# Whole TensorE products cut into four column strips

## The chip, the cores and the metric

The kernel runs on one core of a Trainium2 chip. The metric is device time in microseconds (us), the median over several runs. The core has five engines that work in parallel: TensorE (PE, matrix products, with its own row PEld for the loading of weights), VectorE (DVE), ScalarE (ACT), GpSimd (POOL) and SyncE (SP, which starts transfers). Products land in PSUM, eight banks of 128 partitions by 512 fp32 values; everything else lies in SBUF.

## The reference

For one sequence of 2048 tokens with 512 features, `x`, the output is a gated mix of an attention block and an MLP block:

```python
g = _sigmoid((x * gate_w).sum(-1, keepdims=True))
a = _A_ref(x, A_wqkv, A_wo)                  # 32 heads of 16 features
b = _B_ref(x, B_w1, B_w2, B_w3, B_w4)
return g * a + (1 - g) * b

# _A_ref
scores = jnp.einsum("bhqd,bhkd->bhqk", q, k) * (Dh ** -0.5)
p = _softmax(scores, axis=-1)
o = jnp.einsum("bhqk,bhkd->bhqd", p, v)      # then @ wo

# _B_ref
h = _gelu(_layernorm(x, axis=-1) @ w1)
...                                          # four feature groups shifted by 1, -1, 2, -2 tokens
x1 = x + hs                                  # hs = shifted h @ w2
return x1 + _gelu(_layernorm(x1, axis=-1) @ w3) @ w4
```

## The kernel before

**Attention.** The work is cut into 32 units: four chunks of 512 queries (c) by eight groups of four heads (u). A unit has 64 blocks, one for each of 16 key tiles and four heads. A block is a score product (`score`, L709: 32 rows by 128 columns of the array, four of them beside each other in row tiles), an exp over 128x512 values, and a product with V (`attend_block`, L960: 128 rows by 17 columns, 16 features and a column of ones for the sum, 32 columns wide for the first key tile; four heads beside each other in column tiles of the array, the accumulator `acc` with one head in each quarter of the partitions).

**Who does the exps.** ScalarE does most: a slot is a stage in PSUM of two or three blocks, and one ACTIVATE (`expo`, L947) makes `pt` of it. The rest are done by VectorE with integer arithmetic on the bits of a float, in quads of four blocks (`whole`): a dump of each block out of `dsc` (L873), then the steps L883, L888, L893 and L898 on all four; three terms (`quad`, or a tile borrowed for it such as `more` or `xT`) go into the product with V.

**Whole products.** Everything else on TensorE uses the full array, 128 rows by 128 columns: the projections of q and k (`proj` by `bmm`, L223), of V (`v_proj`, L281), the MLP's four weights and the output projection (`bmm`, L223), the products of the gelu slots (`gelu_slot`, L723) and fills (`fill`, L1259 and L1262), which add zero to an accumulator and are there to be put where TensorE would otherwise have nothing to do.

**Order.** The order of all engines is made when the program is built, by a planner inside the kernel. It keeps an account of when each engine is free (`free`), of what each step costs, and picks the next step by rank and time. For TensorE a product costs `MM` = 0.2235 us, and a product whose kind (`state["kind"]`: score, attend, full) differs from the one before costs `TURN` = 0.09 us more. `fill` is chosen when the next step would start over 0.2 or 0.3 us later. `USUAL` and `RULES` hold, for each unit, when VectorE opens a quad and which unit's it is (NEED, AHEAD, DLIM, CHAINS), when its steps become urgent (HURRY), and when products with V go first (MANY, PTS). `AGE` says how fast a waiting VectorE step gains rank. On the chip each engine runs its list in this order, held together by semaphores, so the times are the chip's and only the order is the planner's.

The first 9 us (warm-up, transposes, first projections) and the last 9 us (`finish_range` and its products, L1106 to L1141) are written out apart from the planner's usual steps.

Of the kernel before, what the change touches and what calls it, by code (L numbers as in the profile page):

```python
# [32 lines left out]
def kernel(  # L33
# [13 lines left out]
    nc = tc.nc  # L47
    P = 128
    x_flat = A_x.flatten_outer_dims()
    out_flat = out.flatten_outer_dims()  # L50
    S, D = x_flat.shape
    H = 32
    DH = D // H
    KT = D // P
# [8 lines left out]
    CH = 512  # L63
# [30 lines left out]
    xT = [const.tile([P, KT, CH], BF16, name=f"xT{c}") for c in range(NC_)]  # L94
    wkv = wshare.tile([P, KT, 2 * D], BF16, tag="wshare", name="wkv")
    wq = const.tile([P, KT, D], BF16, name="wq")
# [7 lines left out]
    zero = const.tile([P, P], BF16, name="zero")  # L104
# [45 lines left out]
    for j in range(4):  # L150
        src = A_wo.rearrange("(G j a d) n -> j a d G n", j=4, a=2, d=DH)[j]
        for a in range(2):
            nc.sync.dma_start(
                out=wo_pad[32 * j + 1:32 * j + 1 + DH, :, :].rearrange("d (G a) n -> a d G n", a=2)[a],
# [3 lines left out]


    USUAL = {"NEED": 34, "AHEAD": 16, "HURRY": 14, "DLIM": 1.8, "MANY": 5, "PTS": 4, "CHAINS": 3}  # L160
    RULES = {1: {"NEED": 26, "HURRY": 0, "MANY": 5, "PTS": 6, "CHAINS": 3}, 2: {"NEED": 26, "HURRY": 0, "DLIM": 1.5, "MANY": 4, "PTS": 5}, 4: {"AHEAD": 16, "HURRY": 8}, 6: {"AHEAD": 6, "HURRY": 0, "DLIM": 2.1, "MANY": 4, "CHAINS": 4}, 7: {"MANY": 3, "PTS": 6}, 8: {"NEED": 26, "HURRY": 18, "CHAINS": 3}, 9: {"NEED": 36, "HURRY": 8, "DLIM": 2.1, "MANY": 3, "CHAINS": 5}, 10: {"DLIM": 1.2, "MANY": 5, "CHAINS": 4}, 12: {"NEED": 26, "HURRY": 18, "MANY": 2}, 13: {"HURRY": 8, "PTS": 5}, 14: {"NEED": 28, "AHEAD": 16, "HURRY": 24, "CHAINS": 5}, 15: {"AHEAD": 10, "MANY": 2, "PTS": 5}, 16: {"NEED": 28, "AHEAD": 16, "DLIM": 1.8, "MANY": 2}, 18: {"NEED": 30, "AHEAD": 6, "HURRY": 0, "MANY": 5}, 19: {"NEED": 32, "DLIM": 1.5}, 20: {"AHEAD": 8, "DLIM": 2.1, "MANY": 4, "PTS": 3, "CHAINS": 4}, 21: {"NEED": 32, "AHEAD": 16, "HURRY": 8, "PTS": 5}, 22: {"AHEAD": 8, "HURRY": 18, "MANY": 3, "PTS": 5}, 23: {"NEED": 30, "AHEAD": 12, "HURRY": 14, "DLIM": 2.1, "CHAINS": 4}, 24: {"NEED": 34, "AHEAD": 8, "MANY": 4, "PTS": 5}, 27: {"AHEAD": 10, "DLIM": 1.8, "CHAINS": 4}, 28: {"NEED": 26, "DLIM": 1.5, "MANY": 4}, 29: {"AHEAD": 10, "DLIM": 1.5, "MANY": 5, "CHAINS": 3}, 30: {"NEED": 28, "AHEAD": 10, "DLIM": 1.5, "MANY": 4}, 31: {"NEED": 32, "HURRY": 18, "MANY": 5, "PTS": 6, "CHAINS": 5}}
    MM = 0.2235
    TURN = 0.09
    PE_OUT = 0.43
    WARM = 8
    EARLY = 34
# [12 lines left out]
    FILL = 2  # L179
    DFILL = 1  # L180
    SLACK = 0.3
    AGE = 2.0
    ARANK = 3
    TANH = 1.5
    NOWFREE = 12.0
    free = {"pe": NOWFREE, "act": NOWFREE, "vector": NOWFREE, "pool": NOWFREE}
    queue = {"pe": [], "act": [], "vector": [], "pool": []}
    state = {"n": 0, "gen": 0, "young": True, "mm": 0, "kind": "", "t": 0.0, "piece": 0.0,
             "credit": 0.0, "mixable": 0, "done": False, "ending": False, "acc": 0.0, "accsb": 0.0, "slot": 0, "outs": 0, "bank": 0}
# [21 lines left out]
    def gen(name, dtype=F32):  # L211
# [5 lines left out]
            return psX.tile([P, CH], dtype, tag="x", name=name)  # L217
        return psG.tile([P, CH], dtype, tag="gen", name=name)

    def bmm(*args, **kwargs):  # L220
        state["mm"] += 1
        state["piece"] += MM
        nc.tensor.matmul(*args, **kwargs)  # L223

    def evac(cost, fn, test=None):

# [48 lines left out]
    def v_proj(t, half):  # L275
        c, o = divmod(t * P, CH)
        heads, width = slice(half * H // 2, (half + 1) * H // 2), D // 2
        yield all_at(("xT", c), "wv")
        ps = gen("ps_v")
        for kt in range(KT):  # L280
            nc.tensor.matmul(ps[:, 0:width], lhsT=xT[c][:, kt, o:o + P], rhs=wkv[:, kt, D + half * width:D + (half + 1) * width],  # L281
                             start=(kt == 0), stop=(kt == KT - 1))
            state["mm"] += 1
            state["piece"] += MM / 2 + 0.01
            if kt == 1:
                yield MM
        dst = vp0 if t == 0 else vp[t - 1]

        def fn(end):
            nc.vector.tensor_copy(out=dst[:, heads, 1:DH + 1], in_=ps[:, 0:width].rearrange("p (h d) -> p h d", d=DH))  # L290
            at["v", t, half] = end

        evac(0.42, fn)
        yield MM
# [283 lines left out]
    def job_run(start, job):  # L578

        if job == "out":  # L580
            job = Job(out_tile(*outs.popleft()))
        elif urgent and job is urgent[0]:
            urgent.popleft()
        state["t"] = start + (TURN if state["kind"] != "full" else 0.0)
        state["piece"] = 0.0
        try:
            v = next(job.steps)
        except StopIteration:
            current["job"] = job.hold = None
            state["done"] = state["done"] or job is main  # L590
            return
        if callable(v):
            current["job"], job.hold = None, v
            return
        current["job"] = job
        if not state["young"]:
            state["credit"] -= v
        free["pe"] = state["t"] + state["piece"]
        state["kind"] = "full"
# [15 lines left out]
    accs, stages, pts, old = {}, {}, {}, {}  # L615
# [97 lines left out]
    def gelu_slot(start):  # L713
        k = len(slots)
        item = turn[k] = gelus.popleft()
        _, _, _, w, rhs, ms, _, _ = item
        stages[k], _ = stage(k, False)
        slots.append([])
        state["slot"] = len(slots)
        state["mm"] = 0  # L720
        for i, m in enumerate(ms):
            for kt in range(KT):
                nc.tensor.matmul(stages[k][:, i * CH:(i + 1) * CH], lhsT=w[:, kt, m * P:(m + 1) * P], rhs=rhs[:, kt, :],  # L723
                                 start=(kt == 0), stop=(kt == KT - 1))
        free["pe"] = start + (TURN if state["kind"] != "full" else 0.0) + len(ms) * KT * MM
        state["kind"] = "full"
        scored[k] = free["pe"] - MM + PE_OUT

    def scores(start):
        k = len(slots)  # L730
        if gelus:
            return gelu_slot(start)
# [250 lines left out]
        return best  # L983

    def attend(start, source):
        begin = start + (TURN if state["kind"] != "attend" else 0.0)
        free["pe"] = begin + MM
        if source is waiting:
            n, kt, members, piece = waiting.popleft()
            if kt == 0:  # L990
                accs[n] = psA.tile([P, CH], F32, tag="acc", name="acc")
                state["acc"] = None
            for m in members:
                k, i = slot_of.pop((n, m) if piece is None else (n, m, piece))
                w = cut.get(k, CH)
                attend_block(n, m, pts[k][:, i * w:(i + 1) * w], r=piece)
                users[k] -= 1
                if users[k] == 0:
                    pt_free[k] = begin + PE_OUT
                    del pts[k]  # L1000
            if piece is not None:
                free["pe"] = begin + MM * w / CH
        else:

            free["pe"] = begin
            n = products[0][0]
            while products and products[0][0] == n and products[0][4] < free["pe"] + 0.02:
                _, kt, heads, term, _, ending = products.popleft()
                for r, j in enumerate(heads):
                    attend_block(n, 4 * kt + j, term.bitcast(BF16)[:, r, :], count=ending)  # L1010
                free["pe"] += MM
                freed[id(term)] = free["pe"] + 0.2
                room.append(term)
                due[n] -= 1
        state["kind"] = "attend"
        if n == len(units) - 1:
            for r in range(len(RANGES)):
                if left[n] == 0 and pieces[r] == 0:
                    pieces[r] = None
                    finish_range(r, free["pe"] - MM + PE_OUT)  # L1020
        elif left[n] == 0:
            finish_unit(n, free["pe"] - MM + PE_OUT)
# [169 lines left out]
    half = CH // 2  # L1192
# [61 lines left out]
    def fill(start):  # L1254

        state["mm"] += 1
        if accs:
            acc = list(accs.values())[0]
            nc.tensor.matmul(acc[:], lhsT=zero[:], rhs=wq[:, 0, :], start=False, stop=False, skip_group_check=True)  # L1259
        else:  # L1260
            spare = psG.tile([P, CH], F32, tag="gen", name="spare")
            nc.tensor.matmul(spare[:], lhsT=zero[:], rhs=wq[:, 0, :], start=True, stop=True)  # L1262
        free["pe"] = start + MM + (TURN if state["kind"] != "full" else 0.0)
        state["kind"] = "full"

    def option(e):
# [47 lines left out]
    while True:  # L1314
        options = []
        o = pe_option()
        if o:
            options.append((o[0], 0, "pe", o))
        for i, e in enumerate(("act", "vector", "pool")):
            o = option(e)  # L1320
# [4 lines left out]
        start, _, e, o = min(options, key=lambda x: x[:2])  # L1325
# [39 lines left out]
```

## Time and profile before

| | |
|---|---|
| median of 3 runs | 805.58 us (805.29 to 805.96) |
| span of the profiled execution | 803.7 us |
| between span and median | 1.9 us; no other time of the profiled execution is given |
| TensorE products, weight loads | 6332 and 6332, busy 773.4 us and 245.8 us |
| VectorE, ScalarE | busy 760.8 us and 787.6 us |
| mean granted TensorE clock | 0.997 |
| first exp starts, last exp ends | 9.0 us, 794.9 us |

How to read it: the page shares out the span by engine, and names the chain of work that ended last. A busy TensorE is no proof of a full one, since the end of a product is modelled and products overlap: what counts is the distance from one start to the next. In a group of instructions, the number behind the second bar is the idle time of the engine just before them, with what ended it.

### The profile page before, as it was taken

How to read it: one execution, taken by the hardware profiler on the slowest of the kernel's cores; microseconds unless marked ns; L12 is line 12 of the kernel's file. 1: busy time of each engine (PE TensorE's matmuls, PEld its weight loads, DVE VectorE, ACT ScalarE, POOL GpSimd, SP SyncE). 2: the span in 40 equal slices, each digit the busy share in tenths (PEclk: the TensorE clock that was granted, in tenths of full speed). 3: DMA queues.
4: the chain of work that ended last, by engine and by line, in shares of the span. 5: the costliest groups of instructions: out<-in, count | busy, mean ns of one | idle time of the engine just before them, and what ended most of it. 6: DMA issues, size and time to landing. Idle time of an engine off the chain costs nothing.

```text
span 803.7 us, 15774 instructions
## 1 busy us (share of the span) xinstructions
PE 773.4 (96%) x6332; PEld 245.8 (31%) x6332; DVE 760.8 (95%) x1237; ACT 787.6 (98%) x734; POOL 19.6 (2%) x46
## 2 busy tenths in 40 slices
PE   9999999999999999999999999999999999999997
PEld 3333333332322323232222233222233233322223
DVE  5799999999889999999999997999999999999995
ACT  6999999999999999999999999999999999999996
POOL 4100000000000000010000000000000000000000
PEclk9999999999999999999999999999999999999998
DMA  8700031230100033001000001001001000000000
GB/s 201 179 15 15 16 67 28 41 42 15 42 1 15 15 106 42 15 1 41 15 14 26 18 15 41 15 3 42 13 14 41 15 6 12 21 21 29 15 15 27
DMA packets 48176, 26.41 MB, mean 33 GB/s; under 512 B 34664, under 2 KB 43624, under 8 KB 48104
## 3 DMA queue, kind: packets, MB, share of 16 engines
q1 hardware_dynamic: 47144, 24.90, 13.0%
q8 instruction: 49, 0.80, 0.4%
q10 hardware_dynamic: 960, 0.52, 0.2%
q14 instruction: 23, 0.19, 0.1%
HBM read 17.04 MB, written 2.35 MB: 24 GB/s over the span
## 4 chain that ended last, share of the span: by engine, by line
ACT 59%; issue 21%; PE 17%; DVE 2%; DVEq 0%; ACTq 0%
ACT pt L947 54%; PE stage L709 5%; PE acc L960 4%; PE ps L223 3%; ACT g2T L925 2%; ACT g2T L928 1%; DVE st L311 1%; ACT L925 1%; PE ps_y L223 1%; PE acc L1259 1%; ACT hT L925 1%; PE ps_v L281 1%; PE ps_k L223 1%; PE warm L1177 0%; PE spare L1262 0%
## 5 line engine op out<-in xcount | busy, mean ns | idle before, releaser
L947 ACT ACTIVATE pt<-stage 128x1024 bf16<-128x1024 f32 (+1 forms) x695 | 738.1, 1236 | 2.6 <-PE stage L709 1.2
L709 PE MATMUL stage<-qT,kT 32*128 32x512 bf16 (+2 forms) x1644 | 270.9, 379 | 22.1 <-ACT pt L947 10.8
L873 DVE TENSOR_SCALAR quad<-dsc 128x512 int16<-128x512 f32 x320 | 213.2, 684 | 13.7 <-PE dsc L709 11.8
L709 PE MATMUL dsc<-qT,kT 32*128 32x512 bf16 x428 | 164.5, 384 | 0.0
L960 PE MATMUL acc<-pt,vp 128*17 128x512 bf16 (+3 forms) x1644 | 157.1, 380 | 1.1 <-ACT pt L947 0.8
L709 PEld LDWEIGHTS <-kT 32*128 32x128 bf16 x2072 | 83.5, 91 | 237.1 <-issue 203.8
L960 PEld LDWEIGHTS <-vp 128*17 128x17 bf16 (+1 forms) x2928 | 60.3, 88 | 131.4 <-issue 119.4
L960 PE MATMUL acc<-quad,vp 128*17 128x512 bf16 x884 | 82.7, 382 | 0.3
L1259 PE MATMUL acc<-wq,zero 128*128 128x512 bf16 x216 | 75.9, 387 | 0.0
L223 PE MATMUL ps<-w,g2T 128*128 128x512 bf16 x224 | 68.4, 384 | 0.8 <-DVE x_sb L433 0.8
L898 DVE TENSOR_SCALAR quad<-quad 128x2048 int16<-128x2048 int16 x80 | 54.2, 679 | 0.3
L223 PE MATMUL ps_y<-xnT,w 128*128 128x512 bf16 x176 | 54.1, 384 | 0.1
L873 DVE TENSOR_SCALAR xT<-dsc 128x512 int16<-128x512 f32 x60 | 40.0, 684 | 0.7 <-PE dsc L709 0.4
L888 DVE TENSOR_TENSOR quad<-quad,quad 128x2048 bf16<-128x2048 bf16 x30 | 36.4, 1213 | 0.3
L883 DVE TENSOR_SCALAR quad<-quad 128x2048 int16<-128x2048 int16 x50 | 34.2, 683 | 0.1
L893 DVE TENSOR_SCALAR quad<-quad 128x2048 int16<-128x2048 int16 x50 | 34.1, 682 | 0.1
L873 DVE TENSOR_SCALAR more<-dsc 128x512 int16<-128x512 f32 x48 | 32.2, 686 | 0.9 <-PE dsc L709 0.2
L1259 PEld LDWEIGHTS <-zero 128*128 128x128 bf16 x216 | 19.1, 96 | 44.8 <-issue 41.6
L223 PEld LDWEIGHTS <-g2T 128*128 128x128 bf16 x224 | 16.9, 97 | 33.1 <-issue 27.5
L723 PE MATMUL stage<-xnT,w 128*128 128x512 bf16 x112 | 25.0, 379 | 0.1
L960 PE MATMUL acc<-more,vp 128*17 128x512 bf16 x248 | 24.3, 382 | 0.0
L1031 DVE COPY accsb<-acc 128x512 f32<-128x512 f32 x31 | 21.2, 684 | 1.6 <-PE acc L960 1.3
(145 smaller groups left out, 682.0 us busy)
## 6 DMA issues: line engine op xcount, KB each, us to landing
bcs<-rec_d SPq DMA_DIRECT2D x31, 256.0 KB
w<-in_B_w_dram SPq DMA_DIRECT2D x2, 1792.0 KB
out_dram<-ot SPq DMA_DIRECT2D x15, 128.0 KB
x_sb<-in_A_x_dram SPq DMA_DIRECT2D x14, 128.0 KB
w<-in_B_w_dram SPq DMA_DIRECT2D x2, 512.0 KB
wkv<-in_A_wqkv_dram SPq DMA_DIRECT2D x1, 512.0 KB
wo_pad<-in_A_wo_dram SPq DMA_DIRECT2D x8, 64.0 KB
xnT<-xn SPq DMA_TRANSPOSE x32
```

The source lines that it names most:

```text
L223: nc.tensor.matmul(*args, **kwargs)
L709: nc.tensor.matmul(out, lhsT=kT[G][32 * j:32 * j + 32, cc, o:o + P], rhs=qTs[(c, G)][32 * j:32 * j + 32, a, lo:hi], start=True, stop=True, ...
L723: nc.tensor.matmul(stages[k][:, i * CH:(i + 1) * CH], lhsT=w[:, kt, m * P:(m + 1) * P], rhs=rhs[:, kt, :], start=(kt == 0), stop=(kt == KT ...
L873: nc.vector.tensor_scalar(out=bits[:, r, :], in0=dsc[:], scalar1=SHIFT, scalar2=LOWEST, op0=ALU.add, op1=ALU.max)
L883: nc.vector.tensor_scalar(out=tiles["once"], in0=bits, scalar1=0x7F, scalar2=0x3F00, op0=ALU.bitwise_and, op1=ALU.bitwise_or)
L888: nc.vector.tensor_tensor(out=tiles["twice"].bitcast(BF16), in0=bits.bitcast(BF16), in1=tiles["once"].bitcast(BF16), op=ALU.mult)
L893: nc.vector.tensor_scalar(out=tiles["once"], in0=bits, scalar1=0x7F80, scalar2=None, op0=ALU.bitwise_and)
L898: nc.vector.tensor_scalar(out=bits, in0=bits, scalar1=QUARTER, scalar2=None, op0=ALU.add)
L925: nc.scalar.activation(out=part, in_=part, func=ACT.Gelu_apprx_tanh)
L947: nc.scalar.activation(out=pt[:, 0:w], in_=stages.pop(k)[:, 0:w], func=ACT.Exp, scale=LN2 / 128.0)
L960: nc.tensor.matmul(accs[n][32 * j:32 * j + M, lo:hi], lhsT=lhsT, rhs=p, start=(kt == 0), stop=(kt == NT - 1), skip_group_check=True, tile_ ...
L1259: nc.tensor.matmul(acc[:], lhsT=zero[:], rhs=wq[:, 0, :], start=False, stop=False, skip_group_check=True)
```

## The change

A new helper `strips` issues a whole product as four products of 32 columns, each with its own 32 columns of weights and its own quarter of the output's partitions, and with the tile position of that column strip. `bmm`, `v_proj`, `gelu_slot` and `fill` use it. The head and the tail keep their whole products, and so do the small gate products. The planner's account then charges no turn between whole products and products with V (`NARROW`), `AGE` is doubled, and some units have other rules. The planner makes a new order of that.

```diff
-    RULES = {... 4: {"AHEAD": 16, "HURRY": 8}, 6: {... "MANY": 4, "CHAINS": 4}, 7: {"MANY": 3, "PTS": 6}, ... 9: {"NEED": 36, ...
+    RULES = {... 4: {"AHEAD": 16, "HURRY": 8, "CHAINS": 6}, 6: {... "MANY": 8, "CHAINS": 2}, 7: {"MANY": 3, "PTS": 6, "CHAINS": 6}, ... 9: {"NEED": 24, ...
...
+    NARROW = ("full", "attend")
...
-    AGE = 2.0
+    AGE = 4.0
...
+    def strips(out, lhsT, rhs, **kwargs):
+
+        for j in range(0, P, 32):
+            nc.tensor.matmul(out[j:j + 32, :], lhsT=lhsT[:, j:j + 32], rhs=rhs, tile_position=(0, j), **kwargs)
+
     def bmm(*args, **kwargs):
         state["mm"] += 1
         state["piece"] += MM
-        nc.tensor.matmul(*args, **kwargs)
+        strips(*args, **kwargs)
...
         for kt in range(KT):                                                     # v_proj
-            nc.tensor.matmul(ps[:, 0:width], lhsT=xT[c][:, kt, o:o + P], ...
+            strips(ps[:, 0:width], lhsT=xT[c][:, kt, o:o + P], ...
...
-        state["t"] = start + (TURN if state["kind"] != "full" else 0.0)          # job_run
+        state["t"] = start + (TURN if state["kind"] not in NARROW else 0.0)
...
             for kt in range(KT):                                                 # gelu_slot
-                nc.tensor.matmul(stages[k][:, i * CH:(i + 1) * CH], lhsT=w[:, kt, m * P:(m + 1) * P], ...
+                strips(stages[k][:, i * CH:(i + 1) * CH], lhsT=w[:, kt, m * P:(m + 1) * P], ...
...
-        begin = start + (TURN if state["kind"] != "attend" else 0.0)             # attend
+        begin = start + (TURN if state["kind"] not in NARROW else 0.0)
...
-            nc.tensor.matmul(acc[:], lhsT=zero[:], rhs=wq[:, 0, :], start=False, ...      # fill
+            strips(acc[:], lhsT=zero[:], rhs=wq[:, 0, :], start=False, ...
```

The rules also change in units 16, 21, 23, 24, 26, 27, 28, 29 and 30 (for example unit 27, AHEAD from 10 to 4). `gelu_slot` and `fill` charge the turn by `NARROW` as well.

More of the change, by code (lines that the diff above doesn't have):

```diff
@@ L160 @@
     USUAL = {"NEED": 34, "AHEAD": 16, "HURRY": 14, "DLIM": 1.8, "MANY": 5, "PTS": 4, "CHAINS": 3}
-    RULES = {1: {"NEED": 26, "HURRY": 0, "MANY": 5, "PTS": 6, "CHAINS": 3}, 2: {"NEED": 26, "HURRY": 0, "DLIM": 1.5, "MANY": 4, "PTS": 5}, 4: {"AHEAD": 16, "HURRY": 8}, 6: {"AHEAD": 6, "HURRY": 0, "DLIM": 2.1, "MANY": 4, "CHAINS": 4}, 7: {"MANY": 3, "PTS": 6}, 8: {"NEED": 26, "HURRY": 18, "CHAINS": 3}, 9: {"NEED": 36, "HURRY": 8, "DLIM": 2.1, "MANY": 3, "CHAINS": 5}, 10: {"DLIM": 1.2, "MANY": 5, "CHAINS": 4}, 12: {"NEED": 26, "HURRY": 18, "MANY": 2}, 13: {"HURRY": 8, "PTS": 5}, 14: {"NEED": 28, "AHEAD": 16, "HURRY": 24, "CHAINS": 5}, 15: {"AHEAD": 10, "MANY": 2, "PTS": 5}, 16: {"NEED": 28, "AHEAD": 16, "DLIM": 1.8, "MANY": 2}, 18: {"NEED": 30, "AHEAD": 6, "HURRY": 0, "MANY": 5}, 19: {"NEED": 32, "DLIM": 1.5}, 20: {"AHEAD": 8, "DLIM": 2.1, "MANY": 4, "PTS": 3, "CHAINS": 4}, 21: {"NEED": 32, "AHEAD": 16, "HURRY": 8, "PTS": 5}, 22: {"AHEAD": 8, "HURRY": 18, "MANY": 3, "PTS": 5}, 23: {"NEED": 30, "AHEAD": 12, "HURRY": 14, "DLIM": 2.1, "CHAINS": 4}, 24: {"NEED": 34, "AHEAD": 8, "MANY": 4, "PTS": 5}, 27: {"AHEAD": 10, "DLIM": 1.8, "CHAINS": 4}, 28: {"NEED": 26, "DLIM": 1.5, "MANY": 4}, 29: {"AHEAD": 10, "DLIM": 1.5, "MANY": 5, "CHAINS": 3}, 30: {"NEED": 28, "AHEAD": 10, "DLIM": 1.5, "MANY": 4}, 31: {"NEED": 32, "HURRY": 18, "MANY": 5, "PTS": 6, "CHAINS": 5}}
@@ new lines @@
+    RULES = {1: {"NEED": 26, "HURRY": 0, "MANY": 5, "PTS": 6, "CHAINS": 3}, 2: {"NEED": 26, "HURRY": 0, "DLIM": 1.5, "MANY": 4, "PTS": 5}, 4: {"AHEAD": 16, "HURRY": 8, "CHAINS": 6}, 6: {"AHEAD": 6, "HURRY": 0, "DLIM": 2.1, "MANY": 8, "CHAINS": 2}, 7: {"MANY": 3, "PTS": 6, "CHAINS": 6}, 8: {"NEED": 26, "HURRY": 18, "CHAINS": 3}, 9: {"NEED": 24, "HURRY": 8, "DLIM": 2.1, "MANY": 3, "CHAINS": 5}, 10: {"DLIM": 1.2, "MANY": 5, "CHAINS": 4}, 12: {"NEED": 26, "HURRY": 18, "MANY": 2}, 13: {"HURRY": 8, "PTS": 5}, 14: {"NEED": 28, "AHEAD": 16, "HURRY": 24, "CHAINS": 5}, 15: {"AHEAD": 10, "MANY": 2, "PTS": 5}, 16: {"NEED": 30, "AHEAD": 16, "DLIM": 1.8, "MANY": 2}, 18: {"NEED": 30, "AHEAD": 6, "HURRY": 0, "MANY": 5}, 19: {"NEED": 32, "DLIM": 1.5}, 20: {"AHEAD": 8, "DLIM": 2.1, "MANY": 4, "PTS": 3, "CHAINS": 4}, 21: {"NEED": 32, "AHEAD": 16, "HURRY": 8, "PTS": 5, "CHAINS": 6}, 22: {"AHEAD": 8, "HURRY": 18, "MANY": 3, "PTS": 5}, 23: {"NEED": 30, "AHEAD": 12, "HURRY": 14, "DLIM": 1.2, "CHAINS": 4}, 24: {"NEED": 34, "AHEAD": 8, "MANY": 5, "PTS": 5}, 26: {"NEED": 36}, 27: {"AHEAD": 4, "DLIM": 1.8, "CHAINS": 4}, 28: {"NEED": 26, "DLIM": 1.5, "MANY": 4, "PTS": 6, "AHEAD": 20}, 29: {"AHEAD": 10, "DLIM": 1.5, "MANY": 5, "CHAINS": 3, "PTS": 4}, 30: {"NEED": 28, "AHEAD": 10, "HURRY": 18}, 31: {"NEED": 32, "HURRY": 18, "MANY": 5, "PTS": 6, "CHAINS": 5}}
@@ L280, in v_proj @@
         for kt in range(KT):
-            nc.tensor.matmul(ps[:, 0:width], lhsT=xT[c][:, kt, o:o + P], rhs=wkv[:, kt, D + half * width:D + (half + 1) * width],
+            strips(ps[:, 0:width], lhsT=xT[c][:, kt, o:o + P], rhs=wkv[:, kt, D + half * width:D + (half + 1) * width],
                              start=(kt == 0), stop=(kt == KT - 1))
@@ L722, in gelu_slot @@
             for kt in range(KT):
-                nc.tensor.matmul(stages[k][:, i * CH:(i + 1) * CH], lhsT=w[:, kt, m * P:(m + 1) * P], rhs=rhs[:, kt, :],
+                strips(stages[k][:, i * CH:(i + 1) * CH], lhsT=w[:, kt, m * P:(m + 1) * P], rhs=rhs[:, kt, :],
                                  start=(kt == 0), stop=(kt == KT - 1))
-        free["pe"] = start + (TURN if state["kind"] != "full" else 0.0) + len(ms) * KT * MM
+        free["pe"] = start + (TURN if state["kind"] not in NARROW else 0.0) + len(ms) * KT * MM
         state["kind"] = "full"
@@ L1258, in fill @@
             acc = list(accs.values())[0]
-            nc.tensor.matmul(acc[:], lhsT=zero[:], rhs=wq[:, 0, :], start=False, stop=False, skip_group_check=True)
+            strips(acc[:], lhsT=zero[:], rhs=wq[:, 0, :], start=False, stop=False, skip_group_check=True)
         else:
             spare = psG.tile([P, CH], F32, tag="gen", name="spare")
-            nc.tensor.matmul(spare[:], lhsT=zero[:], rhs=wq[:, 0, :], start=True, stop=True)
-        free["pe"] = start + MM + (TURN if state["kind"] != "full" else 0.0)
+            strips(spare[:], lhsT=zero[:], rhs=wq[:, 0, :], start=True, stop=True)
+        free["pe"] = start + MM + (TURN if state["kind"] not in NARROW else 0.0)
         state["kind"] = "full"
```

## The prediction

> **What bounds the kernel now.** I read the page first: busy shares and the chain that ended last.
>
> ```profile
> span 803.7 us, 15774 instructions
> ...
> PE 773.4 (96%) x6332; PEld 245.8 (31%) x6332; DVE 760.8 (95%) x1237; ACT 787.6 (98%) x734; POOL 19.6 (2%) x46
> ...
> ACT 59%; issue 21%; PE 17%; DVE 2%; DVEq 0%; ACTq 0%
> ```
>
> Three engines look full, and 38% of the chain (issue 21, PE 17) lies on TensorE, which invites the thought that a cheaper TensorE shortens the run. So next come the stretches between the first and the last exp (the first two windows below are the whole of the head and of the middle), the ACTIVATEs by form, and the waits.
>
> ```profile
> core 0: us, PE busy (x) PEld busy (x) DVE busy (x) ACT busy (x) POOL busy (x), PEclk, DMA share, GB/s
> 0.00:9.00 9.00, 7.70 (x48) 3.93 (x48) 3.65 (x10) 2.64 (x5) 8.10 (x34) 1.00 0.69 179
> 9.00:795.00 786.00, 760.63 (x6258) 239.00 (x6261) 753.21 (x1218) 784.01 (x728) 10.27 (x13) 1.00 0.13 31
> 795.00:803.70 8.70, 5.05 (x30) 2.84 (x29) 3.91 (x11) 0.96 (x2) 1.26 (x1) 0.76 0.17 60
> 486.79:488.40 1.61, 1.61 (x33) 0.71 (x32) 0.01 (x1) 1.61 (x2) 0.00 (x0) 1.00 0.39 127
> 787.25:795.12 7.87, 7.03 (x114) 3.25 (x113) 3.29 (x8) 7.64 (x7) 0.00 (x0) 1.00 0.01 2
> ```
> ```profile
> L947 ACT ACTIVATE pt<-stage 128x1024 bf16<-128x1024 f32 x465 | 441.7, 1095 | 1.9 <-PE stage L709 1.2 <-PE dsc L709 0.2 <-ACT pt L947 0.2
> L947 ACT ACTIVATE pt<-stage 128x1536 bf16<-128x1536 f32 x230 | 321.5, 1519 | 0.7
> ```
> ```profile
> PE stage L709 <- ACT pt L947: 10.8, 38, 0.8
> ```
>
> From 9 to 795 us ScalarE is busy 784.0 of 786.0 us. Before all 695 exps together it stood idle 1.9 + 0.7 = 2.6 us, while TensorE's scores waited 10.8 us for it. ScalarE is the bound, and TensorE follows it. The idle figure is a little low:
>
> ```profile
> 399.40 5.75 ACT L947 ACTIVATE pt<-stage 128x1024 bf16<-128x1024 f32 x6
> ```
>
> Six exps of 1024 columns take 5.75 us; less the last one's 1.10, the starts are 0.93 us apart, though each is 1.10 long. A delay under 0.17 us is thus covered by the overlap and shows nowhere. My estimate of all waits of ScalarE is 4.0 us: the 2.6 of the row and about half as much again of hidden ones. That is everything a faster TensorE can win.
>
> **The change, part by part.** The sum is made against the profiled execution: a span of 803.7 us, with 1.9 us around it up to the runs' median of 805.58. I carry those 1.9 us along and count in medians.
>
> *ScalarE's own work.* Counted in the two programs' instruction lists, the exps stay 695, but 465 of two blocks and 230 of three become 461 and 234: four more blocks on ScalarE, and 107 quads by VectorE become 106. By the rows above a third block costs 1519 - 1095 = 424 ns: 4 x 0.424 = **+1.70 us**, on the path. Gelus and table loads keep their numbers. VectorE gets one quad less, four dumps and four steps,
>
> ```profile
> L873 DVE TENSOR_SCALAR quad<-dsc 128x512 int16<-128x512 f32 x320 | 213.2, 684 | 13.7 <-PE dsc L709 11.8
> L898 DVE TENSOR_SCALAR quad<-quad 128x2048 int16<-128x2048 int16 x80 | 54.2, 679 | 0.3
> L888 DVE TENSOR_TENSOR quad<-quad,quad 128x2048 bf16<-128x2048 bf16 x30 | 36.4, 1213 | 0.3
> ```
>
> 4 x 0.684 + 3 x 0.68 + 1.213 = 6.0 us. It was idle 33 us in the middle, so this gains nothing by itself.
>
> *TensorE's turns.* The timeline of TensorE alone shows what a change of tiling costs:
>
> ```profile
> 399.71 0.39 PE L709 MATMUL stage<-qT,kT 32*128 32x512 bf16 x2
> 399.72 0.38 PE L709 MATMUL dsc<-qT,kT 32*128 32x512 bf16 x1
> 400.03 0.39 PE L960 MATMUL acc<-more,vp 128*17 128x512 bf16 x4
> 400.25 0.39 PE L960 MATMUL acc<-pt,vp 128*17 128x512 bf16 x4
> 400.57 0.39 PE L709 MATMUL stage<-qT,kT 32*128 32x512 bf16 x2
> 400.58 0.38 PE L709 MATMUL dsc<-qT,kT 32*128 32x512 bf16 x1
> 400.89 0.39 PE L960 MATMUL acc<-quad,vp 128*17 128x512 bf16 x4
> 401.22 0.39 PE L223 MATMUL ps<-w,g2T 128*128 128x512 bf16 x1
> 401.54 0.39 PE L709 MATMUL stage<-qT,kT 32*128 32x512 bf16 x2
> ```
> ```profile
> 785.77 0.82 PE L1259 MATMUL acc<-wq,zero 128*128 128x512 bf16 x3
> ```
>
> V after V starts 0.22 us later (400.03 to 400.25); score to V, V to score, V to whole and whole to score each take 0.32 or 0.33 us. Whole after whole is (0.82 - 0.39) / 2 = 0.215 us (785.77). So each turn costs about 0.105 us more than a product of the same tiling. In the lists, neighbours of different tiling number 1758 before; after it 1380, since a strip product and a V product both tile 128x32. That removes 378 x 0.105 = 40 us of TensorE. The list has 64 fills more (288 for 224): 64 x 0.215 = 14 us back. Net about **-26 us of TensorE**, all beside ScalarE's work. TensorE's needs in the lists are, before, 557 us of products (0.216 us each, narrower ones pro rata) and 1758 x 0.106 = 186 us of turns, 744 us; after, 571 + 146 = 717 us, beside ScalarE's 786. Nothing of it counts directly; it counts where TensorE was late for ScalarE. Between two scores TensorE's work, fills left out, exceeded the exp's time (0.92 us for two blocks, 1.34 for three, estimates from the spacing above and the 0.424) in 251 of 683 slots of the list; after the change in 160 of 679, and slots with over 1.3 us of work fall from 64 to 17. The first count says 36% fewer waits, the second 73%. I take half: **-2.0 us** of the 4.0.
>
> *A strip's own price.* No whole product stands in strips in this trace. The nearest rows are V's four tiles, 17 or, for the first block, 32 columns wide:
>
> ```profile
> 67.64 0.61 PE L960 MATMUL acc<-pt,vp 128*32 128x512 bf16 x8
> ```
> ```profile
> 486.79 1.40 PEld L960 LDWEIGHTS <-vp 128*17 128x17 bf16 x32 [0.42 <-issue]
> ```
> ```profile
> L960 PEld LDWEIGHTS <-vp 128*17 128x17 bf16 x2800 | 58.5, 88 | 121.8 <-issue 110.0 <-DVE accsb L1093 0.8 <-DVE st L311 0.5
> L960 PEld LDWEIGHTS <-vp 128*32 128x32 bf16 x128 | 3.4, 93 | 9.6 <-issue 9.4 <-DVE vp L290 0.2
> L223 PEld LDWEIGHTS <-g2T 128*128 128x128 bf16 x224 | 16.9, 97 | 33.1 <-issue 27.5
> ```
>
> Four 32-column tiles and the next four take 0.61 - 0.39 = 0.22 us, like a whole product, loads included. A 32-column load takes 93 ns, a 128-column one 97, and the four stand almost together. I therefore take a strip product at 0.22 us and its four loads at nothing: the running product covers them. If that cover is gone, each product bears up to 0.093 us (a rival). Below nothing it can't go: the same 512 columns stream through every tile.
>
> [...]
>
> *Instructions.* Each of the 1264 strip products (fills among them) issues eight instructions for two; the list grows from 12,664 to 20,360. On average one must leave every 786 / 20,200 = 39 ns. Rows: eight V products in a row, 65 instructions in 1.61 us, or 25 ns each; 227 in 7.87 us, 35 ns each, over the longest dense stretch. Taken at nothing, with the bound as a rival. Waits and semaphore steps stay as many (1451 matmuls wait, 1455 before), and no DMA is added or moved out of its queue by the strips; AGE and the rules only shift when jobs and quads fall. Head and tail (9.0 and 8.7 us) keep their whole products.
>
> Sum: 805.58 + 1.70 - 2.0 = **805.3 us**.
>
> **The rivals.**
>
> *Nearly every wait goes.* If TensorE is never late, all 4.0 us go: 805.58 + 1.70 - 4.0 = 803.3 us. For it: the 26 us freed, and 17 crowded slots for 64. Against: the 160 that stay, and waits at table changes and unit ends that are VectorE's.
>
> *The turn stays* (it ends slower). If strip and V still drain each other, because their loads cannot pass, the 403 strip-V neighbours of the new list bear 0.105 us that its account leaves out: 42 us, TensorE at 759 of 786. Still not the bound on average, but late in the crowded slots: 160 x 403/679 x 0.105 = 10 us of lateness, of which I let half reach ScalarE past its second buffer: with +1.70, 812 us. It decides from the point where ScalarE's waits do not shrink at all, 807.3 us. For it: 17 columns next to whole strips isn't in the trace. Against: 32-column V next to 17-column V runs without a turn.
>
> *The issue of instructions binds.* At 40 ns each, 20,360 take 814 us, and with head and tail 832 us. It decides above 39 ns. Against: 25 and 35 ns in the rows; for it: both stretches are short, and instructions queued ahead may flatter them. [...]
>
> *Loads are not covered.* 1264 x 0.093 = 118 us on TensorE, 717 + 118 = 835, with head and tail 853 us. It decides when over (786 - 717) / 1264 = 55 ns of each are exposed. Against: the V rows.
>
> **How the numbers follow.** Some of the waits go, 805.3 us: 0.41, its own range 804.0 to 807.1. Nearly all go: 0.27. The turn stays, or the new order makes ScalarE wait as long as before or longer: 0.20. Issue binds: 0.09. Loads uncovered: 0.03. What a measurement here can tell from no change is about 0.2%, 1.6 us: 804.0 to 807.2. So faster 0.27, same 0.41, slower 0.20 + 0.09 + 0.03 = 0.32. The range 803.0 to 811.0 takes in the second case and most of the third, and leaves out the last two and the third's upper end.
>
> **What would show it.** Right: strip to V and V to strip 0.22 us apart; strip to strip 0.22; TensorE's scores waiting more than 10.8 us for exps; ScalarE's idle before the exps under 2.6 us; ScalarE's middle stretch near 786 us again. Wrong: strip to V at 0.32 (the turn stays), strip to strip above 0.25 with loads starting late (issue or loads), or idle before the exps of 4 us and more with PE as its releaser. If the exps' idle falls to nearly nothing and the span is still near 804, the bound was read rightly and the gain simply had no room.

## The result, and the profile after

The changed kernel takes 812.93 us (median; 811.68 to 813.63) where the kernel before took 805.77 us beside it: a ratio of 1.0086 [1.0073 to 1.0099], about 7 us slower. The profiled execution of after took 813.63 us. The lines below answer to those of before. First the page: span, busy shares with the number of instructions, and the chain that ended last.

```profile
span 811.7 us, 23471 instructions
...
PE 767.6 (95%) x10180; PEld 267.8 (33%) x10180; DVE 757.6 (93%) x1229; ACT 789.7 (97%) x734; POOL 19.1 (2%) x46
...
ACT 60%; issue 22%; PE 15%; DVE 2%; DMA 0%; DVEq 0%; ACTq 0%
```

TensorE's busy time fell by 6 us although it now issues 3800 products more, and VectorE's by 3 us. The span grew by 8.0 us. Next the stretches up to the first exp, between the first and the last, and after it, and one dense stretch.

```profile
core 0: us, PE busy (x) PEld busy (x) DVE busy (x) ACT busy (x) POOL busy (x), PEclk, DMA share, GB/s
0.00:9.53 9.53, 8.31 (x48) 4.64 (x48) 3.55 (x10) 2.63 (x4) 8.63 (x35) 1.00 0.72 187
9.53:803.85 794.32, 755.56 (x10102) 261.07 (x10103) 750.03 (x1209) 786.15 (x728) 9.19 (x11) 1.00 0.13 31
803.85:811.70 7.85, 3.78 (x31) 2.09 (x30) 4.04 (x12) 0.96 (x2) 1.27 (x1) 1.00 0.19 67
15.66:81.77 66.11, 64.01 (x1000) 25.55 (x1001) 60.71 (x127) 65.87 (x67) 4.35 (x6) 1.00 0.29 81
```

The middle is 8.3 us longer than before's 786.0. In it ScalarE is busy 2.1 us more and idle 8.2 us instead of 2.0: it worked a little more and waited much more. Where it waited stands in the groups of ScalarE by shape (behind the second bar: the idle time ahead of the group, and what ended most of it) and in a row of the waits (us in total, times, the longest).

```profile
L953 ACT ACTIVATE pt<-stage 128x1024 bf16<-128x1024 f32 x461 | 439.9, 1113 | 2.7 <-PE stage L715 1.1 <-PE dsc L715 0.9
L953 ACT ACTIVATE pt<-stage 128x1536 bf16<-128x1536 f32 x234 | 328.3, 1550 | 1.8 <-PE acc L966 1.0 <-PE stage L715 0.6
L953 ACT ACT_TABLE_LOAD x5 | 6.4, 1283 | 3.3 <-PE dsc L715 3.3
```
```profile
PE stage L715 <- ACT pt L953: 22.9, 86, 0.9
```

Read this row beside the idle times. TensorE's scores waited 22.9 us for exps, twice the 10.8 of before, so on the whole TensorE had more room. Yet ScalarE stood idle 4.5 us before its exps (2.6 before), and 3.3 us once ahead of a table load. An average of room and a wait at one place are different things.

Since idle time hides delays under the overlap of two ACTIVATEs (0.17 us in the six exps at 399.40 of before: starts 0.93 us apart, each 1.10 long), I also worked the waits out from the ends of neighbouring ACTIVATEs: the distance from end to end less 0.917 us for two blocks and 1.343 us for three, the median distances in before's trace; for other ACTIVATEs, less the shortest such distance of before. Then the span is the first exp's start, plus a floor (the exps at those two prices, and the rest), plus the waits, plus the tail behind the last exp:

| | before | after | difference |
|---|---|---|---|
| first exp starts | 8.99 | 9.53 | +0.54 |
| floor: 465 + 230 exps, now 461 + 234 | | | +1.70 |
| waits between exps | 4.4 | 6.6 | +2.2 |
| wait at the gate's copy, 220.8 us | 0 | 1.3 | +1.3 |
| wait ahead of the table load, 233.0 us | 0 | 3.2 | +3.2 |
| tail behind the last exp | 8.85 | 7.85 | -1.0 |

Together 7.9 of the 8.0 us; the rest is rounding. The floor was foreseen. The 6.7 us of new waits were not.

Part of them goes with TensorE's clock. The granted clock (the column PEclk, the share of full speed that TensorE was given) is 0.996 over the whole of after's execution and 0.997 over before's, but in after two stretches of 3.4 us ran at half of it, and in before the same stretches ran at 1.00:

```profile
183.60:187.02 3.42, 3.36 (x30) 0.85 (x33) 2.61 (x5) 2.69 (x3) 0.00 (x0) 0.50 0.02 2
221.15:224.56 3.41, 3.37 (x33) 1.42 (x37) 0.98 (x3) 3.40 (x3) 0.00 (x0) 0.50 0.02 5
```

The longest wait between exps, 1.1 us at 187.3, stands right behind the first. The second lies ahead of the table load's wait, which is followed back further below.

Now the strips themselves, in TensorE alone (a row xN of strips is N/4 whole products):

```profile
395.74 0.39 PE L966 MATMUL acc<-pt,vp 128*17 128x512 bf16 x4
395.95 0.60 PE L224 MATMUL acc<-wq,zero 128*32 128x512 bf16 x8
...
406.56 0.39 PE L715 MATMUL stage<-qT,kT 32*128 32x512 bf16 x3
406.88 0.62 PE L224 MATMUL acc<-wq,zero 128*32 128x512 bf16 x8
407.32 0.39 PE L966 MATMUL acc<-quad,vp 128*17 128x512 bf16 x4
```

V to strip takes 0.21 us (395.74 to 395.95), strip after strip 0.60 - 0.39 = 0.21, two strip products and then V 0.44 (406.88 to 407.32): no turn between strips and V, 32 and 17 columns wide. Score to strip still takes 0.32 us (406.56 to 406.88). So the mechanism of the change is there as written.

### The profile page after: what moved, and what is told of

The parts are those of the page before. It is cut to its first block, busy times and chain, and to the rows that moved or that the text cites. A ratio compares the mean times of both kernels' runs of the same rounds, so it can differ in the third digit from the quotient of the medians.

```text
span 811.7 us, 23471 instructions
## 1 busy us (share of the span) xinstructions
PE 767.6 (95%) x10180; PEld 267.8 (33%) x10180; DVE 757.6 (93%) x1229; ACT 789.7 (97%) x734; POOL 19.1 (2%) x46
## 4 chain that ended last, share of the span: by engine, by line
ACT 60%; issue 22%; PE 15%; DVE 2%; DMA 0%; DVEq 0%; ACTq 0%
ACT pt L953 56%; PE stage L715 4%; PE acc L966 4%; PE ps L224 2%; ACT g2T L931 2%; ACT g2T L934 1%; PE acc L224 1%; PE stage L224 1%; ACT L931 1%; DVE quad L879 1%; PE ps_o L224 0%; PE ps_v L224 0%; PE warm L1183 0%; PE ps_y L224 0%; DMA xnT<-xn 0%
## 5 line engine op out<-in xcount | busy, mean ns | idle before, releaser
L715 PE MATMUL stage<-qT,kT 32*128 32x512 bf16 (+2 forms) x1648 | 272.0, 379 | 31.0 <-ACT pt L953 22.9
L879 DVE TENSOR_SCALAR quad<-dsc 128x512 int16<-128x512 f32 x304 | 202.0, 684 | 22.9 <-PE dsc L715 21.0
L224 PE MATMUL acc<-wq,zero 128*32 128x512 bf16 x1116 | 98.3, 383 | 0.0
L224 PE MATMUL ps<-w,g2T 128*32 128x512 bf16 x896 | 66.9, 382 | 0.1
L224 PE MATMUL ps_y<-xnT,w 128*32 128x512 bf16 x704 | 54.7, 388 | 0.9 <-DVE g2T L360 0.6
L879 DVE TENSOR_SCALAR more<-dsc 128x512 int16<-128x512 f32 x76 | 50.3, 684 | 1.6 <-PE dsc L715 1.2
L894 DVE TENSOR_TENSOR quad<-quad,quad 128x2048 bf16<-128x2048 bf16 x41 | 49.8, 1216 | 0.2
L224 PEld LDWEIGHTS <-w 128*32 128x32 bf16 x1152 | 29.4, 97 | 36.3 <-issue 18.1
L224 PEld LDWEIGHTS <-zero 128*32 128x32 bf16 x1216 | 30.5, 94 | 31.9 <-issue 23.6
L224 PE MATMUL stage<-xnT,w 128*32 128x512 bf16 x448 | 26.7, 397 | 3.3 <-DMA xnT<-xn 2.4
L224 PEld LDWEIGHTS <-g2T 128*32 128x32 bf16 x896 | 19.4, 95 | 22.3 <-issue 13.2
```

Of the source, the lines that this page charges most:

```text
L224: nc.tensor.matmul(out[j:j + 32, :], lhsT=lhsT[:, j:j + 32], rhs=rhs, tile_position=(0, j), **kwargs)
L715: nc.tensor.matmul(out, lhsT=kT[G][32 * j:32 * j + 32, cc, o:o + P], rhs=qTs[(c, G)][32 * j:32 * j + 32, a, lo:hi], start=True, stop=True, ...
L879: nc.vector.tensor_scalar(out=bits[:, r, :], in0=dsc[:], scalar1=SHIFT, scalar2=LOWEST, op0=ALU.add, op1=ALU.max)
L894: nc.vector.tensor_tensor(out=tiles["twice"].bitcast(BF16), in0=bits.bitcast(BF16), in1=tiles["once"].bitcast(BF16), op=ALU.mult)
```

## The experiments

The theory after the result: strips do what they promise, and what costs the time is the new order that the planner made along with them. The rival: strips cost ScalarE time in a way that the matmul rows don't show, whatever the order. So first each half alone.

**Strips in the old order.** Before, with the four uses of `strips`; account, AGE and RULES stay, so every engine's list is the old one but for the strips.

```diff
-        nc.tensor.matmul(*args, **kwargs)        # bmm; likewise v_proj, gelu_slot, fill
+        strips(*args, **kwargs)
```

> The order of before, word for word, with the whole products issued as strips (account, AGE and rules of before). Theory 'order': strips are no dearer than whole products and turns vanish, so TensorE gains about 40 us of room and ScalarE's waits shrink from 4.1 us: 803.0 to 805.6 us, strip to V starts 0.22 us apart. Theory 'strips': the strips themselves are what costs (loads, issue, or stalls at scores): 808 to 813 us.

Measured: 805.47 us beside 805.48, ratio 0.999 [0.998 to 1.0]. ScalarE by shape, and the scores' wait for it:

```profile
L952 ACT ACTIVATE pt<-stage 128x1024 bf16<-128x1024 f32 x465 | 444.6, 1139 | 2.0 <-PE stage L714 1.2 <-PE dsc L714 0.7
L952 ACT ACTIVATE pt<-stage 128x1536 bf16<-128x1536 f32 x230 | 325.1, 1558 | 1.0 <-PE stage L714 0.8
```
```profile
PE stage L714 <- ACT pt L952: 26.0, 113, 0.7
```

TensorE gained room: its scores wait 26.0 us for exps instead of 10.8. ScalarE's idle time before exps is 3.0 us (2.6 before), and by the rule of the table above its waits are 4.3 us (4.4 before; the expectation puts them at 4.1). The rival falls: strips cost nothing here. A gain is not clear of the noise: the interval leaves room for up to 1.6 us, and the mean of the 12 runs is 0.9 us below that of the 17 runs of before.

The equal sums hide a trade. Set against each other exp by exp, waits of before shrink by 1.8 us in all, at 17 exps, as was hoped for. And 1.8 us come anew at four exps: 0.8 us at 209 and 212 us, in and behind a stretch at half clock, 0.8 us at 322 us, where TensorE had waited for a transpose, and 0.2 us at 327 us:

```profile
207.03:210.44 3.41, 3.41 (x34) 0.92 (x26) 2.18 (x4) 2.85 (x3) 0.00 (x0) 0.50 0.41 79
```
```profile
321.31 0.40 PE L223 MATMUL ps_y<-xnT,w 128*32 128x512 bf16 x4 [0.95 <-DMA xnT<-xn]
```

In this execution strips did win the small waits, and other delays took their place. Whether these belong to the strips or to this one execution was not shown.

**Whole products in the new order.** After, with the loop in `strips` replaced by one product.

```diff
-        for j in range(0, P, 32):
-            nc.tensor.matmul(out[j:j + 32, :], lhsT=lhsT[:, j:j + 32], rhs=rhs, tile_position=(0, j), **kwargs)
+        nc.tensor.matmul(out, lhsT=lhsT, rhs=rhs, **kwargs)
```

> The order of after, word for word, with whole products instead of strips. Theory 'order': the 3.3 us and 1.3 us that ScalarE loses around the first gelu (217 to 233 us of the span) stay, and the turns that the account left out come back, 403 x 0.105 = 42 us of TensorE: 813 us or more, up to 825. Theory 'strips': 803 to 808 us, since only the order is left and it has TensorE better placed.

Measured: 822.17 us, ratio 1.0191 [1.0169 to 1.0212].

```profile
L952 ACT ACTIVATE pt<-stage 128x1024 bf16<-128x1024 f32 x461 | 440.4, 1060 | 9.0 <-PE dsc L714 5.7 <-PE stage L714 1.4 <-PE acc L965 0.2
L952 ACT ACTIVATE pt<-stage 128x1536 bf16<-128x1536 f32 x234 | 324.6, 1493 | 2.4 <-PE stage L714 1.6 <-PE acc L965 0.5
```

Idle before exps is 11.4 us against 4.5 with strips, and TensorE's scores are named for 8.7 of it (5.7 + 1.4 + 1.6). By ends of ACTIVATEs all the waits come to 20.8 us against 11.1, which accounts for the 9 us between the two runs. The new order is 17 us worse than the old one with whole products, and strips win back about half of that. They are worth 9 us there and at most 1.6 in the old order: a cheaper TensorE pays only where TensorE is late.

**Which part of the account makes the order worse?** After with the RULES and AGE of before, so that only strips and `NARROW` remain; and after with AGE alone set back.

```diff
-    RULES = {... of after}
-    AGE = 4.0
+    RULES = {... of before}
+    AGE = 2.0
```

> Strips and the account without turns between strips and V, but AGE and RULES of before; the planner makes a third order. Theory 'order', rules and AGE are to blame: 803 to 807 us. Theory 'order', the account itself is to blame (it packs TensorE closer): 810 us or more. Theory 'strips': 808 to 813 us.

```diff
-    AGE = 4.0
+    AGE = 2.0
```

> After with AGE back at 2.0. If the slower ageing of VectorE's waiting steps put the last normalisation and the gate's copy late (g_raw was taken behind five quad steps at 220.63 us): 805 to 809 us. If it is the rules or the account: 811 to 815 us.

Measured: 819.53 us, 1.0164 [1.0148 to 1.0181], and 829.78 us, 1.0284 [1.0265 to 1.0304]. The account without the new rules is worse than the change as a whole, and the new rules without the new AGE worse still. The 829.78 us lie far outside both ranges that were given for this run. So the rules and AGE of after belong together, and the change as a whole is 7 us better than strips and account alone. Their waits, with ScalarE as the one that waits, first of the account with old rules, then of AGE 2:

```profile
ACT pt L953 <- PE acc L966: 4.8, 3, 2.3
```
```profile
ACT pt L953 <- PE acc L966: 9.7, 3, 6.9
ACT L953 <- PE dsc L715: 8.7, 1, 8.7
```

These waits are few and long: three of 4.8 us together in the one, three of 9.7 and one of 8.7 in the other. The first kind is seen at 266 us in the account with old rules, where a unit changes:

```profile
265.47 0.69 DVE L1037 COPY accsb<-acc 128x512 f32<-128x512 f32 x1
...
266.21 0.83 PE L966 MATMUL acc<-pt,vp 128*32 128x512 bf16 x12 [0.80 <-DVE accsb L1037]
...
266.69 1.02 ACT L953 ACTIVATE pt<-stage 128x1024 bf16<-128x1024 f32 x1 [2.26 <-PE acc L966]
```

The next unit's products with V wait for VectorE's copy of the accumulator, the `pt` tiles stay taken, and ScalarE has nowhere to write. Here TensorE itself waits, so its pace does not enter.

**Is it this account, or any new order?** Before, with TURN moved by 0.001 us, which is a hundredth of a turn; and before with AGE alone doubled.

```diff
-    TURN = 0.09
+    TURN = 0.091
```

> Before with its account's turn at 0.091 us for 0.09, nothing else: whole products, old AGE and rules. Theory 'any new order': the rules fit one order alone, and a change of the account by a thousandth of a microsecond makes the planner write another, without that fit: 812 to 825 us. Theory 'the account without turns': only the removal of the turn from the account, 0.09 us at 403 places, packs TensorE too close; then this stays at 804 to 808 us.

```diff
-    AGE = 2.0
+    AGE = 4.0
```

> Before with AGE at 4.0 and nothing else. If the doubled AGE is good for the chip by itself (after gets 17 us slower without it), 803 to 806 us. Theory 'any new order': it was only good for the order it was fitted to, and here it loses: 812 to 822 us.

Measured: 817.59 us, 1.0148 [1.0127 to 1.0169], and 839.37 us, 1.0415 [1.0393 to 1.0436]. TURN 0.091 describes the chip as well as 0.09 does (the rows of before gave about 0.105 us), and costs 12 us:

```profile
L947 ACT ACTIVATE pt<-stage 128x1024 bf16<-128x1024 f32 x469 | 447.1, 1086 | 7.5 <-PE dsc L709 4.4 <-PE stage L709 2.3
L947 ACT ACTIVATE pt<-stage 128x1536 bf16<-128x1536 f32 x226 | 315.9, 1508 | 5.9 <-PE acc L960 2.9 <-PE stage L709 2.6
```

13.4 us of idle before exps instead of 2.6. The doubled AGE alone costs 34 us, far more than either range that was given for it. So both steps off the order of before lose much, also where nothing was taken out of the account. My reading is that its RULES fit that one order; how they were found is not on record, and two steps are not every step. The strips in the order of TURN 0.091, with its lists unchanged:

```diff
-    TURN = 0.09                                  # in the kernel with strips in the old order
+    TURN = 0.091
```

> The order of before_turn091 (whole products, turn 0.091 us in the account: 817.59 us, ScalarE waits 18 us) with strips for whole products. In that order the neighbours of whole and V products lose their turn of 0.105 us each, about 40 us of TensorE, and no engine's list changes. Theory 'room': strips win only where TensorE is late, and here it is, by small waits of ScalarE on it: 808 to 814 us, as 822.2 became 812.9 us in the new order. Theory 'stalls': the waits come from late VectorE terms and transposes and not from TensorE's pace: 816 to 818 us.

Measured: 813.83 us, 1.0098 [1.0082 to 1.0115], so strips win about 4 us.

```profile
L952 ACT ACTIVATE pt<-stage 128x1024 bf16<-128x1024 f32 x469 | 448.5, 1117 | 5.7 <-PE dsc L714 3.3 <-PE stage L714 1.9
L952 ACT ACTIVATE pt<-stage 128x1536 bf16<-128x1536 f32 x226 | 318.3, 1542 | 5.3 <-PE acc L965 2.9 <-PE stage L714 2.0
```

The idle ended by scores shrinks (`dsc` 4.4 to 3.3, `stage` 4.9 to 3.9 over both rows), the 2.9 us ended by `acc` stays to the digit: strips help the first kind of wait and not the second.

**The largest wait of after.** Its 3.2 us at 233.0 were followed back. SyncE's queue in after, and then in before (start of an issue, and how long SyncE was taken up by it; the data land later: in after the last transpose is issued by 214.44 + 5.15 = 219.59, and TensorE's wait for them ends at 221.19):

```profile
210.78 0.32 SPq L1050 DMA_DIRECT2D rec_d<-rec  x1
213.79 0.54 SPq L1051 DMA_DIRECT2D bcs<-rec_d  x1
214.44 5.15 SPq L350 DMA_TRANSPOSE xnT<-xn  x4
```
```profile
206.90 5.16 SPq L344 DMA_TRANSPOSE xnT<-xn  x4
212.11 0.59 SPq L1044 DMA_DIRECT2D rec_d<-rec  x1
```

In before the transposes of `xn` go ahead of the two transfers of the sums' reciprocals; in after they stand behind them. `bcs` reads what `rec_d` has written and so holds the queue until 213.79, and the transposes start at 214.44, though their last input was there at 211.83 + 0.41 = 212.24. That row of VectorE, and what then happens, by the timeline of after:

```profile
211.83 0.41 DVE L337 TENSOR_SCALAR xn<-x_sb,mv,rstd 128x512 bf16<-128x512 bf16 x1
...
221.19 5.28 PE L224 MATMUL stage<-xnT,w 128*32 128x512 bf16 x64 [2.39 <-DMA xnT<-xn]
...
227.86 1.91 ACT L934 ACTIVATE hT<-stage 128x1024 bf16<-128x1024 f32 x2
...
228.83 0.40 PE L966 MATMUL acc<-quad,vp 128*17 128x512 bf16 x4 [0.20 <-DVE quad L894]
...
230.50 2.12 PE L224 MATMUL acc<-wq,zero 128*32 128x512 bf16 x36
...
232.55 0.39 PE L715 MATMUL stage<-qT,kT 32*128 32x512 bf16 x2
...
233.03 1.28 ACT L953 ACT_TABLE_LOAD   x1 [3.25 <-PE dsc L715]
```

TensorE waits 2.39 us for the transposes. The 16 whole products behind them, 64 strips, take 5.28 us, since from 221.15 to 224.56 the clock is at half (the second of the two rows at 0.50 in the section on the result). TensorE's list then holds products with V that wait for VectorE's terms, and nine fills, 2.0 us, which were meant to fill a gap and now stand in front of a score. That score comes at 232.55, while ScalarE is done with the gelus at 227.86 + 1.91 = 229.77. The test: the two transfers by GpSimd's queue.

```diff
-            nc.sync.dma_start(out=rd.rearrange(...), in_=rec[:])
-            nc.sync.dma_start(out=bcs[:], in_=rd.unsqueeze(1).to_broadcast([4, 32, CH]))
+            nc.gpsimd.dma_start(out=rd.rearrange(...), in_=rec[:])
+            nc.gpsimd.dma_start(out=bcs[:], in_=rd.unsqueeze(1).to_broadcast([4, 32, CH]))
```

> After with the two transfers of a unit's reciprocals (rec_d and bcs) started by GpSimd instead of SyncE; the order on all engines stays. In after the four transposes of the last first-layer chunk stood in SyncE's queue behind bcs, which waited for rec_d, until 214.44 us, though their data were ready at 212.24; TensorE then waited 2.4 us for them, and ScalarE 3.3 us before its next exp. Theory 'queue': the transposes start 2.2 us earlier, and 2 to 4 us come back: 809 to 811.5 us. Theory 'plan': the order has TensorE behind two gelu slots and ten fills there in any case: 812 to 814 us.

Measured: 812.15 us, ratio 1.0082 [1.0065 to 1.0099], not to be told from after. Yet the wait is gone, so the time lies in the range of theory 'plan' though its reason did not hold:

```profile
208.00 5.81 SPq L350 DMA_TRANSPOSE xnT<-xn  x4
...
219.14 3.64 PE L224 MATMUL stage<-xnT,w 128*32 128x512 bf16 x64
```
```profile
L953 ACT ACT_TABLE_LOAD x5 | 6.4, 1283 | 0.1
```

By SyncE's queue (first line) the transposes start 6.4 us earlier, and the idle time ahead of the table loads falls from 3.3 to 0.1 us. The place was read rightly, but two delays went together: TensorE no longer waits, and no half clock follows, so the same 64 strips take 3.64 us instead of 5.28. The queue alone does not make the whole wait. With whole products in the same order the transposes stood behind `bcs` too, TensorE waited 1.42 us for them, the clock stayed full there, and ScalarE's wait ahead of the table load was 0.6 us:

```profile
222.06 3.61 PE L223 MATMUL stage<-xnT,w 128*128 128x512 bf16 x16 [1.42 <-DMA xnT<-xn]
...
232.44 1.28 ACT L952 ACT_TABLE_LOAD   x1 [0.61 <-PE dsc L714]
```

In the run with GpSimd's queue, GpSimd issues `bcs` 1.6 us later than SyncE did (213.79),

```profile
215.43 0.71 POOL L1051 DMA_DIRECT2D bcs<-rec_d  x1 [3.03 <-DMA rec_d<-rec]
```

and by the ends of ACTIVATEs the waits between exps grow from 6.6 to 8.6 us: 3.2 won, 2.0 given back. The waits' sum falls from 11.1 to 9.9 us. Half of the 2.0, at 509 and 511 us, stands right behind another stretch at half clock, 505.37 to 508.78, where after had 1.00. That the later `bcs` brings the rest was not shown.

**Rules fitted anew.** If only the fit is lost, new rules for the new account might bring it back. Two sets of RULES were chosen so that the planner's own account of the whole program came out shortest, with strips, `NARROW` and AGE 4.0.

```diff
-    RULES = {... of after}
+    RULES = {... chosen by the planner's account}
```

> After with other rules for its units: strips, the account without turns and AGE 4.0 stay, and the rules are chosen anew so that the planner's own order ends earlier, with 1644 blocks on ScalarE as before. Theory 'fit': the 7 us were the rules' poor fit to the new account, and a fitted order is back at the level of before: 802 to 808 us. Theory 'account': an order without turns packs TensorE too close for the chip whatever the rules: 810 us or more.

> As strips_fitted_1, with a second set of rules found from another start. Theory 'fit': 802 to 808 us. Theory 'account': 810 us or more. If the two differ by more than 3 us, what the planner doesn't account for (SyncE's queue above all) decides between orders that it holds equal.

Measured: 815.78 us, 1.013 [1.0109 to 1.0151], and 817.91 us, 1.015 [1.0134 to 1.0165]: slower than after, and outside the range of theory 'fit'. The two differ by 2.1 us, under the 3 us named. The first set's waits, and two rows of its SyncE queue:

```profile
ACT pt L953 <- PE dsc L715: 9.8, 5, 3.7
PE ps_y L224 <- DMA xnT<-xn: 6.2, 2, 3.7
```
```profile
295.31 0.42 SPq L472 DMA_DIRECT2D w<-in_B_w_dram  x1
295.78 10.02 SPq L350 DMA_TRANSPOSE xnT<-xn  x4
```

Five waits cost ScalarE 9.8 us. TensorE waits twice for transposes of this kind, 6.2 us together, and behind each of these waits the clock is at half (0.50 from 128.12 to 131.53 and from 309.03 to 312.44). The four transposes shown stand right behind a transfer of weights and take up SyncE for 10.0 us, where the four of after took 5.15. The planner's account takes a fixed time for them and knows nothing of SyncE's queue, so an order that is best in its account can be a bad one on the chip. Whether rules chosen by times on the chip would bring strips below 805 us was not tried.

No version beat the kernel before by more than the noise. Strips in the old order equal it within 0.2%.

## Why the prediction was wrong

The forecast was 805.3 us, with a range up to 811.0; it came to 812.9. Step by step:

- **What bounds the kernel** was right. ScalarE is the bound before and after, and 22 + 15% of the chain on TensorE (issue and PE) meant nothing then and means nothing now. That a cheaper TensorE has little room to pay is what the strips in the old order show, 0.999 [0.998 to 1.0].
- **ScalarE's own work, +1.70 us**, was right: 461 and 234 exps were run, and by the spacings of the trace the floor grew by 4 x (1.343 - 0.917) = 1.70 us.
- **TensorE's turns** were right as a mechanism. Strip and V follow each other at 0.22 us, and the scores' wait for exps doubled.
- **The price of the new order** is the step that failed. The sentence "AGE and the rules only shift when jobs and quads fall" put it at nothing in the sum, without a reason from a row. Measured, the new order costs 17 us with whole products and 7 with strips, the 1.7 us of the floor within.
- **The -2.0 us of waits** did not come. In the old order, where strips gave TensorE the most room, the small waits did shrink by 1.8 us, close to the term, but as much came back at other places, and the sum went from 4.4 to 4.3. In the new order it rose to 11.1. The count of crowded slots (251 to 160) compares TensorE's work with ScalarE's time slot by slot. It knows no queue, no transfer, no VectorE term and no clock, and the long waits of after come from these: a transpose behind a transfer and then half clock, a copy of the gate behind VectorE's steps, fills in front of a score.
- **A strip's own price, 0.22 us with loads at nothing**, was right. A load of 32 columns takes 94 ns, and four of them stay hidden behind a product, with 0.21 us from strip to strip:

```profile
L224 PEld LDWEIGHTS <-zero 128*32 128x32 bf16 x1216 | 30.5, 94 | 31.9 <-issue 23.6
```

- **Instructions** did not bind, as forecast. The nine fills at 230.50 leave (2.12 - 0.39) / 32 = 54 ns for a product with its load, and 2001 of TensorE's instructions went through the 66.11 us shown first, 33 ns each, with ScalarE busy 65.87 of them.
- **The rivals.** *Issue*, *loads* and *nearly every wait goes* fell. *The turn stays, or the new order makes ScalarE wait as long as before or longer* was written with two halves and priced, at 812 us, by the first. The first half did not happen, the second did, and the point from which it was to decide (waits that do not shrink, 807.3 us) was passed. That the sum came out beside the measured 812.9 is chance. Nothing in the trace of before bounded what a new order costs; such a term wants a wide range upwards, and had no price of its own.

By the signs named beforehand: strips at 0.22 us and scores waiting over 10.8 us were met; idle before the exps under 2.6 us and a middle near 786 us were not (4.5 and 794.3). "Idle of 4 us and more with PE as its releaser" was put down as a sign against, and it came: 4.5 us, 3.6 of it with PE named.

Open is which of the rules brings which wait, what decides when the clock falls to half, and whether the head's +0.54 us has to do with the change; the executions here started their first exp anywhere from 8.86 to 9.88 us.

## What to carry to other kernels

Where a planner makes the order, a change of its account is two changes: the cheaper step, and a new order. Try the cheaper step in the old order first; here that one run says that there were at most 1.6 us to win. Take a constant that moves by a hundredth of its size as a measure of how much of the time is only the fit of an order: 12 us here, more than the 7 us of the change. And look for the granted clock stretch by stretch: 3.4 us at half clock made the same 64 strips take 5.28 us instead of 3.64, while the mean clock of the two executions hardly differs (0.996 and 0.995).

## What the runs showed of the hardware

- In after, products 32 columns wide and products 17 columns wide followed each other without a turn, 0.21 to 0.22 us from start to start, while from a score, with 32 rows, to either of them took 0.32 us (396.54 to 396.86 to V, 406.56 to 406.88 to a strip).
- The tail was longest where the granted clock was lowest. The stretch behind the last exp, by windows, first in after's execution (shown above: 7.85 us at 1.00) and here in that of the account with old rules:

```profile
807.54:817.30 9.76, 6.07 (x31) 3.63 (x32) 3.99 (x11) 0.96 (x3) 1.26 (x1) 0.53 0.16 55
```

The same products take 6.07 us instead of 3.78 and the tail 1.9 us more at a clock of 0.53. Before's profiled execution had 0.76 and 8.7 us there, whole products in the new order 1.00 and 7.87 us, strips in the old order 0.87 and 7.82 us. So I put the -1.0 us of the table above down to the clock of two executions and not to the change.
- The clock also fell to half in the middle of a run, for 3.4 us at a time: twice in after (from 183.60 and 221.15 us), once with strips in the old order (207.03), once with GpSimd's queue (505.37) and twice with the first set of fitted rules (128.12 and 309.03). Ahead of the two stretches of after, TensorE was busy 1.02 of 3.41 us (217.74 to 221.15) and 2.06 of 3.41 (180.19 to 183.60). But behind another stretch of after with 2.13 of 3.41 us (535.18 to 538.59) the clock stayed at 1.00, so a quiet TensorE alone is not shown to be the cause.
- Four transposes took up SyncE for 5.16 us in before and 5.15 us in after, and for 10.0 us behind a transfer of weights with the first set of fitted rules. In after, a transfer that waited for another one held the four behind it in SyncE's queue until 214.44 us; with both transfers in GpSimd's queue the first of the four started at 208.00.
